# A fused attention and two-expert-stage kernel whose second stage forms y w1 by one level of Strassen's recursion

## The chip, the cores and the metric

One core of a Trainium2 chip runs one program. The metric is device time in microseconds (us) from the program's first to its last instruction, as the median of timed runs; smaller is better. The engines are TensorE (PE, with its weight loads as PEld), VectorE (DVE), ScalarE (ACT), GpSimd (POOL) and the DMA queue of SyncE (SP).

## What the kernel must compute

Attention in chunks makes x (1536 tokens by 512). A gated block turns x into another 1536 by 512 matrix, called y here, and four experts then work on every token:

```python
def _moe_ref(x, w_gate, w_val, w_out):
    gate = 1.0 / (1.0 + np.exp(-(x @ w_gate)))
    return gate * (x @ w_val) @ w_out                 # 512 -> 1536 -> 512

def _moe2_ref(x, domain_probs, w1, w2):               # x here is y; w1 is [4, 512, 1024], w2 [4, 1024, 512]
    p = domain_probs / (domain_probs.sum(-1, keepdims=True) + 1e-09)
    for e in range(4):
        h = np.maximum(x @ w1[e], 0.0)
        out += p[:, e:e + 1] * (h @ w2[e])
```

Every float32 operand of a large product is split into hi + lo, each exact in float32r, and a product is three matmuls: hi hi, hi lo and lo hi.

## The kernel before

The program has one order, written out by hand for each engine; nothing is rescheduled. It has three stages. In the first, attention is made in blocks of 384 tokens, with pieces of x w_val between its steps; TensorE's matmuls for these write a tile named pv of 384 columns. In the second, x w_gate (tile pg) and the rest of x w_val are made in steps of 512 tokens, and then the product with w_out: for each of three 512-token steps four PSUM tiles pb, one for each 128 columns of y, stand open at once, and for each of 12 pieces of the inner dimension every one of them gets three matmuls. ACT and DVE then split pb into the four y tiles ys (hi and lo, all 1536 tokens). During the third of these steps they also split the first expert's w1.

The third stage is the experts. For each expert and each 512-token step, h_unit (line 481) is called 8 times: 12 matmuls of 512 columns (4 pieces of the inner dimension by 3) add up in one PSUM tile ph, ACT writes the relu's hi part and DVE its lo part. Then o_unit (line 493) is called for 4 groups of 128 tokens: 24 matmuls of 512 columns (8 by 3) add up in a PSUM tile po, and DVE multiplies it by the expert's weight of each token and adds it to acc, one SBUF tile for each of the 12 token groups. The last token group is made in two halves of 256 columns, so that less is left behind the last matmul. The helper mm3 (line 160) issues every one of these triples, so their rows stand on lines 161 to 163 and are told apart by their tiles.

PSUM has 8 banks, given out in turn by ps_tile. Weights come by DMA on SP's queue into four raw tiles of 512 KB (rawp), from which ACT (hi) and DVE (lo) write them into 12 places (wp) for w1 and 10 (wp2) for w2.

## Time and profile before

| | |
|---|---|
| median of 3 runs | 893.57 us (892.66 to 893.98) |
| span of the profiled execution | 893.9 us |
| TensorE busy, share of the span | 870.0 us, 97% |
| DVE, ACT, POOL busy | 315.1, 231.4 and 18.8 us |
| mean granted TensorE clock | 0.996 |

The profiled execution has no time of its own beside its span; the span is 0.3 us above the median and inside the range of the runs, so no offset stands between them. A busy TensorE is one with a matmul in flight: the matmuls overlap, so a matmul's own duration (0.39 us for 512 columns) is longer than the distance from one start to the next, and it is that distance that adds up to the time.

### The profile page before, as it was taken

The page shows a single profiled execution, that of the slowest core. Times are in us where ns is not written, and L with a number is a line of the kernel's source. Part 1 is how long each engine was busy: PE and PEld are TensorE (multiplying, and loading weights), DVE is VectorE, ACT ScalarE, POOL GpSimd, SP SyncE. Part 2 cuts the span into 40 slices and gives each one's busy share as a digit, 9 for nine tenths or more (in the row PEclk, how much of TensorE's full clock was granted, in tenths as well). Part 3 has the DMA queues.
Part 4 walks back from the last instruction along what each step waited for, and adds up shares of the span by engine and source line. Part 5 has one row for each costly group of instructions (what it writes and reads, how often), then busy time and mean ns, then how long its engine had stood idle before and what let it go on. Part 6 is the DMA issues. An engine that isn't in the chain of part 4 may idle for free.

```text
span 893.9 us, 10956 instructions
## 1 busy us (share of the span) xinstructions
PE 870.0 (97%) x4607; PEld 723.7 (81%) x4607; DVE 315.1 (35%) x550; ACT 231.4 (26%) x479; POOL 18.8 (2%) x23
## 2 busy tenths in 40 slices
PE   6689999999999999999999999999999999999998
PEld 3578998888888888888888888888888888888887
DVE  5565366652453334331114322123322123412121
ACT  4455445432232334321112211012201012302020
POOL 2211000000000000000000000000000000000000
PEclk9999999999999999999999999999999999999999
DMA  9999333320220002120002110002110002000101
GB/s 216 246 253 252 102 99 118 114 65 30 71 71 23 1 1 71 47 71 1 1 0 88 51 52 1 0 1 95 48 47 1 1 1 95 0 36 12 48 0 48
DMA packets 19168, 55.35 MB, mean 62 GB/s; under 512 B 2592, under 2 KB 4912, under 8 KB 19120
## 3 DMA queue, kind: packets, MB, share of 16 engines
q1 hardware_dynamic: 19088, 54.63, 21.3%
q8 instruction: 36, 0.59, 0.3%
q14 instruction: 12, 0.10, 0.0%
q0 software_dynamic: 32, 0.02, 0.0%
HBM read 51.50 MB, written 3.15 MB: 61 GB/s over the span
## 4 chain that ended last, share of the span: by engine, by line
PE 91%; DMA 8%; SPq 1%; issue 0%; DVE 0%
PE po L161 10%; PE po L163 10%; PE po L162 10%; PE ph L161 10%; PE ph L162 10%; PE ph L163 10%; DMA kb<-in_kw_dram 4%; PE pb L163 4%; PE pb L161 4%; PE pb L162 4%; PE pg L163 4%; PE pg L161 4%; PE pg L162 4%; PE pv L161 3%; PE pv L163 3%; PE pv L162 3%
## 5 line engine op out<-in xcount | busy, mean ns | idle before, releaser
L488 ACT ACTIVATE h<-ph 128x512 fp32r<-128x512 f32 x96 | 57.4, 598 | 414.4 <-PE ph L163 414.4
L163 PE MATMUL po<-w,h 128*128 128x512 f32 (+1 forms) x392 | 151.0, 385 | 0.0
L162 PE MATMUL po<-w,h 128*128 128x512 f32 (+1 forms) x392 | 151.0, 385 | 0.0
L161 PE MATMUL po<-w,h 128*128 128x512 f32 (+1 forms) x392 | 151.0, 385 | 0.0
L163 PE MATMUL ph<-ys,w 128*128 128x512 f32 x384 | 149.6, 390 | 0.0
L161 PE MATMUL ph<-ys,w 128*128 128x512 f32 x384 | 149.6, 389 | 0.0
L162 PE MATMUL ph<-ys,w 128*128 128x512 f32 x384 | 149.6, 389 | 0.0
L489 DVE SCALAR_TENSOR_TENSOR h<-ph,h 128x512 fp32r<-128x512 f32 x96 | 66.4, 692 | 184.3 <-ACT h L488 184.3
L161 PEld LDWEIGHTS po<-w,h 128*128 128x128 f32 x392 | 73.7, 188 | 14.7
L163 PEld LDWEIGHTS po<-w,h 128*128 128x128 f32 x392 | 73.7, 188 | 14.7
L162 PEld LDWEIGHTS po<-w,h 128*128 128x128 f32 x392 | 73.7, 188 | 14.6
L163 PEld LDWEIGHTS ph<-ys,w 128*128 128x128 f32 x384 | 72.1, 188 | 15.0
L161 PEld LDWEIGHTS ph<-ys,w 128*128 128x128 f32 x384 | 72.1, 188 | 15.0
L162 PEld LDWEIGHTS ph<-ys,w 128*128 128x128 f32 x384 | 72.1, 188 | 14.9
L505 DVE SCALAR_TENSOR_TENSOR acc<-po,p_sb,acc 128x512 f32<-128x512 f32 (+1 forms) x37 | 27.2, 736 | 152.3 <-PE po L163 152.3
L161 PE MATMUL pv<-xs,w_v 128*128 128x384 f32 (+1 forms) x176 | 64.1, 364 | 0.2 <-ACT g L317 0.2
L163 PE MATMUL pv<-xs,w_v 128*128 128x384 f32 (+1 forms) x176 | 61.8, 351 | 0.0
L162 PE MATMUL pv<-xs,w_v 128*128 128x384 f32 (+1 forms) x176 | 61.6, 350 | 0.0
L163 PE MATMUL pb<-hl,w_o 128*128 128x512 f32 x144 | 57.1, 397 | 0.0
L161 PE MATMUL pb<-hl,w_o 128*128 128x512 f32 x144 | 57.1, 397 | 0.0
L162 PE MATMUL pb<-hl,w_o 128*128 128x512 f32 x144 | 57.1, 397 | 0.0
L163 PE MATMUL pg<-xs,w_g 128*128 128x512 f32 x144 | 56.1, 390 | 0.0
(72 smaller groups left out, 910.1 us busy)
## 6 DMA issues: line engine op xcount, KB each, us to landing
raw<-in_w_dram SPq DMA_DIRECT2D x32, 512.0 KB, 3.5
vb<-in_vw_dram SPq DMA_DIRECT2D x32, 195.0 KB, 7.9
kb<-in_kw_dram SPq DMA_DIRECT2D x32, 192.0 KB, 7.6
raw<-in_w_v_dram SPq DMA_DIRECT2D x12, 512.0 KB, 8.6
raw<-in_w_g_dram SPq DMA_DIRECT2D x12, 512.0 KB, 4.4
raw<-in_w_o_dram SPq DMA_DIRECT2D x12, 512.0 KB, 3.4
q<-in_qT_dram SPq DMA_DIRECT2D x16, 192.0 KB, 7.3
out_dram<-acc SPq DMA_DIRECT2D x11, 256.0 KB, 2.0
```

What stands on the lines that cost most here:

```text
L161: nc.tensor.matmul(out=ps, lhsT=w_hi, rhs=r_hi, start=first, stop=False)
L162: nc.tensor.matmul(out=ps, lhsT=w_hi, rhs=r_lo, start=False, stop=False)
L163: nc.tensor.matmul(out=ps, lhsT=w_lo, rhs=r_hi, start=False, stop=last)
L488: nc.scalar.activation(out=h[:, 0], in_=ps, func=AF.Relu)
L489: nc.vector.scalar_tensor_tensor(out=h[:, 1], in0=ps, scalar=0.0, in1=f32(h[:, 0]), op0=ALU.max, op1=ALU.subtract)
L505: nc.vector.scalar_tensor_tensor(out=a, in0=ps[:, n], scalar=p, in1=a, op0=ALU.mult, op1=ALU.add)
```

## The change

The product y w1 of each expert is made by one level of Strassen's recursion (in Winograd's form). The quarters of y are 384 tokens by 256, those of w1 are 256 by 256, and seven products of sums of quarters take the place of eight. Tokens go in two rounds of 768, and w1 and w2 in 16 pieces: a block is one round with one half of an expert's w1 and w2. There are 16 blocks (15 loads of a piece: the round change keeps its piece), and each has two units (128 of the 256 columns of the quarters). A unit makes seven products of 6 matmuls of 384 columns in three PSUM tiles b, e and a: some products add to a tile whose earlier value ACT has just copied out (held), and DVE adds such copies to later tiles (total) to get three of the four quarters of h; the fourth is made in finish, later. Then the block's second product runs as 12 parts of 6 matmuls of 512 columns into six PSUM tiles d; the last part of a block is put into the next block's first unit (prev).

The sums of w1's quarters are made on POOL, in place in the raw tiles (w1_prep: 4 sums), and ACT and DVE split seven tiles of 512 columns for a piece of w1 and four for a piece of w2. They are issued in steps (hooks) between the parts of the block before. The sums of y's quarters are made on POOL too (y_sums), and seven splits of 768 columns follow for each round (y_prep, y_prep_late).

```diff
-    def mm3(ps, w_hi, w_lo, r_hi, r_lo, first, last):
-        nc.tensor.matmul(out=ps, lhsT=w_hi, rhs=r_hi, start=first, stop=False)
-        nc.tensor.matmul(out=ps, lhsT=w_hi, rhs=r_lo, start=False, stop=False)
-        nc.tensor.matmul(out=ps, lhsT=w_lo, rhs=r_hi, start=False, stop=last)
+    def mm3(ps, w_hi, w_lo, r_hi, r_lo, first, last, more=False):
+        nc.tensor.matmul(out=ps, lhsT=w_hi, rhs=r_hi, start=first, stop=False, skip_group_check=more)
+        nc.tensor.matmul(out=ps, lhsT=w_hi, rhs=r_lo, start=False, stop=False, skip_group_check=more)
+        nc.tensor.matmul(out=ps, lhsT=w_lo, rhs=r_hi, start=False, stop=last, skip_group_check=more)
...
+    blocks = [(0, e, g) for e in range(NE) for g in range(NGR)]
+    blocks += [(1, e, g) for e in reversed(range(NE)) for g in reversed(range(NGR))]
+    groups = [b[1:] for b in blocks[:NE * NGR]] + [b[1:] for b in blocks[NE * NGR + 1:]]
+    group_of = [n if n < NE * NGR else n - 1 for n in range(len(blocks))]
...
+    def in_turn(splits):
+        his, los = zip(*splits)
+        return [his[0]] + [both(h, l) for h, l in zip(his[1:], los)] + [los[-1]]
...
+    def w1_prep(n):
+        t = {}
...
+        def hi(m, a):
+            def do():
+                w = wp.tile([128, 2, 2, GW], F32R, tag="w", name=f"w1_{n}_{m}")
+                ops1[n][m] = w
+                nc.scalar.copy(out=w[:, 0], in_=t[a])
+            return do
...
+        def lo(m, a):
+            def do():
+                w = ops1[n][m]
+                nc.vector.tensor_tensor(out=w[:, 1], in0=t[a], in1=f32(w[:, 0]), op=ALU.subtract)
+            return do
+        def comb(dst, a, b, op):
+            return lambda: nc.gpsimd.tensor_tensor(out=t[dst], in0=t[a], in1=t[b], op=op)
...
+        s1 = comb("a22", "a21", "a22", ALU.add)
+        s3 = comb("a21", "a11", "a21", ALU.subtract)
+        s2 = comb("a11", "a22", "a11", ALU.subtract)
+        s4 = comb("a12", "a12", "a11", ALU.subtract)
+        return [
+            both(start, hi(4, "a22"), hi(1, "a11")), both(lo(4, "a22"), s1), both(hi(2, "a12"), lo(1, "a11"), s3, s2),
+            both(lo(2, "a12"), s4), hi(7, "a21"), both(hi(6, "a11"), lo(7, "a21")), both(hi(5, "a22"), lo(6, "a11")),
+            both(hi(3, "a12"), lo(5, "a22")), both(lo(3, "a12"), lambda: raw1_to(n + 3))]
...
+        h, l = ([fn(u, fh) for u in range(2) for fh in range(2)] for fn in (hi, lo))
+        return [both(h[0], h[1], l[0]), both(h[2], l[1]), l[2], h[3], l[3]]
...
+    def y_sums(j, into, eng):
+        y = yr[j]
+        q = {(k, t): y[:, 2 * k:2 * k + 2, t * HT:(t + 1) * HT] for k in range(2) for t in range(2)}
+        d = {(k, t): into[:, 2 * k:2 * k + 2, t * HT:(t + 1) * HT] for k in range(2) for t in range(2)}
+        t1, t3, t2, t4 = d[0, 0], d[0, 1], d[1, 1], d[1, 0]
+        sub = ALU.subtract
+        return (q, dict(t1=t1, t3=t3, t2=t2, t4=t4), dict(
+            t1=combine(eng, t1, q[0, 1], q[0, 0], sub), t3=combine(eng, t3, q[1, 1], q[0, 1], sub),
+            t2=combine(eng, t2, q[1, 1], t1, sub), t4=combine(eng, t4, q[1, 0], t2, sub)))
...
+        def start():
+            q, t, do = y_sums(j, yr[j], nc.gpsimd)
+            h1, l1 = y_split(1, q[0, 0])
+            h3, l3 = y_split(3, q[1, 1])
+            h2, l2 = y_split(2, q[1, 0])
+            h5, l5 = y_split(5, t["t1"])
+            h7, l7 = y_split(7, t["t3"])
+            h6, l6 = y_split(6, t["t2"])
+            h4, l4 = y_split(4, t["t4"])
+            out.extend([
+                [h1], [h3, l1, do["t1"], do["t3"]], [h2, l3, do["t2"]], [h5, l2, do["t4"]],
+                [h7, l5], [h6, l7], [h4, l6], [l4]])
...
+    def y_prep_late(j):
+        q, t, _ = y_sums(j, yr[0], nc.gpsimd)
+        return in_turn([
+            y_split(1, q[0, 0]), y_split(7, t["t3"]), y_split(6, t["t2"]), y_split(2, q[1, 0]),
+            y_split(4, t["t4"]), y_split(5, t["t1"]), y_split(3, q[1, 1])])
...
+        def product(n, u, m, ps, first):
+            w, y = ops1[group_of[n]][m], yops[0][m]
+            fc = slice(u * 128, (u + 1) * 128)
+            for k in range(2):
+                mm3(ps[:, :HT], w[:, 0, k, fc], w[:, 1, k, fc], y[:, 0, k], y[:, 1, k], first and k == 0, k == 1,
+                    not first)
...
+        def total(name, ps, s):
+            v = small(name, 4)
+            nc.vector.tensor_tensor(out=v, in0=ps[:, :HT], in1=s, op=ALU.add)
+            return v
+        def held(ps):
+            s = small("s", 6)
+            nc.scalar.copy(out=s, in_=ps[:, :HT])
+            return s
...
+        def unit(n, u, prev):
+            b, e = ps_tile(f"b{n}_{u}"), ps_tile(f"e{n}_{u}")
+            product(n, u, 1, b, True)
+            s1 = held(b)
+            product(n, u, 7, e, True)
+            s7 = held(e)
+            a = None
+            if prev is None:
+                a = ps_tile(f"a{n}_{u}")
+                product(n, u, 2, a, True)
+            else:
+                prev()
+            product(n, u, 6, b, False)
+            s2 = held(b)
+            if a is None:
+                a = ps_tile(f"a{n}_{u}")
+                product(n, u, 2, a, True)
+            hook()
+            c11 = total("v", a, s1)
+            h_hi(n, u, (0, 0), c11)
+            product(n, u, 4, e, False)
+            c21 = total("v", e, s2)
+            h_lo(n, u, (0, 0), c11)
+            h_hi(n, u, (1, 0), c21)
+            product(n, u, 5, b, False)
+            c22 = total("v", b, s7)
+            h_lo(n, u, (1, 0), c21)
+            h_hi(n, u, (1, 1), c22)
+            h_lo(n, u, (1, 1), c22)
+            hook()
+            def finish():
+                product(n, u, 3, b, False)
+                h_hi(n, u, (0, 1), b[:, :HT])
+                h_lo(n, u, (0, 1), b[:, :HT])
+            return finish
...
+        def o_part(n, d, tt, u, first, last, cols):
+            th, c = divmod(tt, RT // 2)
+            c = slice(c * 128, (c + 1) * 128)
+            for fh in range(2):
+                h, w = H2[n, u, (fh, th)], ops2[group_of[n], u, fh]
+                mm3(d[:, cols], h[:, 0, c], h[:, 1, c], w[:, 0, cols], w[:, 1, cols],
+                    first and fh == 0, last and fh == 1)
+                hook(keep=2)
...
+        for n in range(len(blocks)):
+            end = n == len(blocks) - 1
+            if n == 2:
+                for do in y_sums(1, yr[0], nc.gpsimd)[2].values():
...
+            fin0 = unit(n, 0, prev)
+            if n == 0:
+                hook(2)
+            fin1 = unit(n, 1, fin0)
+            hook(len(hooks))
+            if n == NE * NGR - 1:
+                hooks.extend(y_prep_late(1))
+            elif not end:
+                g = group_of[n + 1]
+                hooks.extend(w1_prep(g) + w2_prep(g))
+            ds, waiting = {}, []
+            def part(tt, u, d_first=0, d_last=1):
...
+            part(0, 0)
+            part(1, 0)
+            fin1()
+            part(2, 0)
+            part(3, 0)
+            part(0, 1)
+            part(1, 1)
+            flushed(0)
+            part(2, 1)
+            flushed(1)
+            part(3, 1)
+            flushed(2)
+            part(4, 0)
+            flushed(3)
+            part(4, 1)
+            if not end:
+                part(5, 0)
+                flushed(4)
...
+                def prev(n=n, ds=ds):
+                    o_part(n, ds[5], 5, 1, False, True, ALL)
+                    flush(n, ds[5], 5, ALL)
+            else:
...
+                if c == NCT - 1:
+                    y_steps, w_steps = y_prep(0), w1_prep(0)
                 for f in range(KF):
...
-                    if c == NCT - 1 and n_w < n_64 + KE:
-                        split_f32(wp, n_w)
-                        n_w += 1
+                    if c == NCT - 1:
+                        emit(y_steps, 1)
+                        emit(w_steps, 1 if f >= 2 else 0)
...
+                    yr.extend(xp.tile([128, KD, 2 * HT], F32, tag="x", name=f"yr{j}") for j in range(NR))
+                    yops.extend(y_ops())
                 for m in range(KD):
-                    if c == 0:
-                        y_t[m] = xp.tile([128, 2, B * S], F32R, tag="x", name=f"ys{m}")
-                    put_split(y_t[m][:, 0, ct(c)], y_t[m][:, 1, ct(c)], pss[m])
...
+                    for j in range(NR):
+                        t0, t1 = max(c * CT, j * 2 * HT), min((c + 1) * CT, (j + 1) * 2 * HT)
+                        if t0 < t1:
+                            nc.scalar.copy(
+                                out=yr[j][:, m, t0 - j * 2 * HT:t1 - j * 2 * HT], in_=pss[m][:, t0 - c * CT:t1 - c * CT])
```

Place 1, TensorE. The first expert unit. In the kernel before, the twelve matmuls of a tile ph stand together; four of them from the second tile on, with their y tiles ys:

```order
L163 MATMUL ph0_0_0_3359<-ys3_2921,w_1_0_0_3135 128x512
L161 MATMUL ph0_0_1_3378<-ys0_2912,w_1_0_1_3153 128x512
L162 MATMUL ph0_0_1_3378<-ys0_2912,w_1_0_1_3153 128x512
L163 MATMUL ph0_0_1_3378<-ys0_2912,w_1_0_1_3153 128x512
L161 MATMUL ph0_0_1_3378<-ys1_2915,w_1_0_1_3153 128x512
```

In the changed kernel, at the end of block 0's first unit (b0_0, e0_0: PSUM tiles of block 0, unit 0; yo4, yo5, yo1: operands made from y; w1_0_5: the fifth product's operand made from w1):

```order
L152 MATMUL e0_0_3381<-yo4_2924,w1_0_4_3180 128x384
L150 MATMUL b0_0_3380<-yo5_2925,w1_0_5_3298 128x384 [waits Activation_49]
L151 MATMUL b0_0_3380<-yo5_2925,w1_0_5_3298 128x384
L152 MATMUL b0_0_3380<-yo5_2925,w1_0_5_3298 128x384 [waits DVE_49]
L150 MATMUL b0_0_3380<-yo5_2925,w1_0_5_3298 128x384
L151 MATMUL b0_0_3380<-yo5_2925,w1_0_5_3298 128x384
L152 MATMUL b0_0_3380<-yo5_2925,w1_0_5_3298 128x384
L150 MATMUL b0_1_3451<-yo1_2919,w1_0_1_3182 128x384 [waits PE_49]
```

A tile changes every 6 matmuls instead of every 12, the tile b0_0 is one that matmuls had written before, and the matmul that returns to it waits for ACT (the copy held).

Place 2, ACT. In the kernel before, in the second token step of the first expert, ACT has one relu for each tile ph and nothing between them:

```order
L488 ACTIVATE h0_1_0_3636<-ph0_1_0_3623 128x512 [waits PE_49]
L488 ACTIVATE h0_1_1_3652<-ph0_1_1_3639 128x512 [waits DVE_49,PE_49]
L488 ACTIVATE h0_1_2_3668<-ph0_1_2_3655 128x512 [waits DVE_49,PE_49]
L488 ACTIVATE h0_1_3_3684<-ph0_1_3_3671 128x512 [waits DVE_49,PE_49]
L488 ACTIVATE h0_1_4_3700<-ph0_1_4_3687 128x512 [waits DVE_49,PE_49]
```

In the changed kernel, from the second product of block 0 to the first unit of block 1 (w1_1_4: fourth product's operand of piece 1, w2_1_0_0: a piece of w2, s: the copies held):

```order
L223 CAST w1_1_2_3542<-raw1_1_0_2912 128x512
L361 ACTIVATE h0_1_(0, 1)_3558<-b0_1_3451 128x384 [waits PE_49]
L223 CAST w1_1_7_3565<-raw1_1_1_2914 128x512 [waits Pool_49]
L223 CAST w1_1_6_3570<-raw1_1_0_2912 128x512 [waits Pool_49]
L223 CAST w1_1_5_3577<-raw1_1_1_2914 128x512
L223 CAST w1_1_3_3583<-raw1_1_0_2912 128x512 [waits Pool_49]
L251 CAST w2_1_0_0_3597<-raw2_1_0_3494 128x512 [waits DMAHW4_49]
L251 CAST w2_1_0_1_3599<-raw2_1_1_3496 128x512 [waits DMAHW5_49]
L251 CAST w2_1_1_0_3605<-raw2_1_0_3494 128x512
L375 COPY s_3657<-b1_0_3649 128x384 [waits PE_49,Activation_49]
```

Three splits now wait for POOL, and the copy that TensorE waits for stands behind them.

Place 3, POOL. In the kernel before its last tensor work is in the first stage. In the changed kernel these rows are the four sums of one piece of w1, each in place in a raw tile:

```order
L233 TENSOR_TENSOR raw1_1_1_2914<-raw1_1_1_2914 128x512 [waits DMAHW3_49,DMAHW7_49,DMAHW2_49,DVE_49]
L233 TENSOR_TENSOR raw1_1_1_2914<-raw1_1_0_2912,raw1_1_1_2914 128x512 [waits DMAHW6_49,Pool_49]
L233 TENSOR_TENSOR raw1_1_0_2912<-raw1_1_1_2914,raw1_1_0_2912 128x512 [waits DMAHW2_49,DVE_49,Pool_49]
L233 TENSOR_TENSOR raw1_1_0_2912<-raw1_1_0_2912 128x512 [waits DVE_49,Pool_49]
```

They follow each other as a chain: each one after the first waits for POOL's own earlier sum, and the first waits for DVE, which has to have read the raw tile.

## Rows read from the trace of the kernel before

**Rows 1.** The page's first part: busy time, share of the span, instructions.
```profile
PE 870.0 (97%) x4607; PEld 723.7 (81%) x4607; DVE 315.1 (35%) x550; ACT 231.4 (26%) x479; POOL 18.8 (2%) x23
```

**Rows 2.** Busy time of each engine by stretch, granted clock, DMA share, GB/s.
```profile
core 0: us, PE busy (x) PEld busy (x) DVE busy (x) ACT busy (x) POOL busy (x), PEclk, DMA share, GB/s
...
119.83:136.12 16.29, 16.29 (x95) 16.29 (x95) 15.05 (x29) 10.13 (x20) 0.00 (x0) 1.00 0.54 161
136.12:266.72 130.60, 130.60 (x577) 108.16 (x577) 64.61 (x109) 45.64 (x79) 0.00 (x0) 1.00 0.24 77
266.72:368.16 101.44, 101.44 (x434) 81.67 (x433) 38.58 (x59) 31.57 (x54) 0.00 (x0) 1.00 0.08 26
368.16:890.69 522.53, 522.49 (x2328) 433.62 (x2326) 136.73 (x202) 86.67 (x153) 0.00 (x0) 1.00 0.09 30
```

**Rows 3.** The page's chain that ended last, by engine.
```profile
PE 91%; DMA 8%; SPq 1%; issue 0%; DVE 0%
```

**Rows 4.** Groups of TensorE's matmuls by tile and shape: count, busy, mean ns.
```profile
L163 PE MATMUL ph<-ys,w 128*128 128x512 f32 x384 | 149.6, 390 | 0.0
...
L163 PE MATMUL po<-w,h 128*128 128x512 f32 x376 | 146.5, 390 | 0.0
...
L163 PE MATMUL pb<-hl,w_o 128*128 128x512 f32 x144 | 57.1, 397 | 0.0
...
L162 PE MATMUL po<-w,h 128*128 128x256 f32 x16 | 4.5, 284 | 0.0
```

**Rows 5.** TensorE's instructions in order of time: start us, us.
```profile
119.83 0.33 PE L163 MATMUL pv<-xs,w_v 128*128 128x384 f32 x1
...
120.35 0.33 PE L163 MATMUL pv<-xs,w_v 128*128 128x384 f32 x1
...
136.12 0.39 PE L161 MATMUL pg<-xs,w_g 128*128 128x512 f32 x1
...
266.72 0.40 PE L161 MATMUL pb<-hl,w_o 128*128 128x512 f32 x1
...
367.93 0.39 PE L161 MATMUL ph<-ys,w 128*128 128x512 f32 x1
...
846.66 0.39 PE L161 MATMUL ph<-ys,w 128*128 128x512 f32 x1
...
868.42 0.39 PE L161 MATMUL po<-w,h 128*128 128x512 f32 x1
...
884.74 0.28 PE L161 MATMUL po<-w,h 128*128 128x256 f32 x1
...
890.38 0.28 PE L163 MATMUL po<-w,h 128*128 128x256 f32 x1
```

**Rows 6.** Groups of ACT's instructions by shape: count, busy, mean ns, idle before.
```profile
L111 ACT CAST w<-raw 128x512 fp32r<-128x512 f32 x64 | 37.3, 615 | 13.4 <-PE pb L163 13.4
...
L317 ACT COPY g<-pv 128x384 f32<-128x384 f32 x32 | 15.1, 484 | 30.7 <-PE pv L163 30.5
```

**Rows 7.** The same of DVE.
```profile
L112 DVE TENSOR_TENSOR w<-raw,w 128x512 fp32r<-128x512 f32 x64 | 42.0, 684 | 12.2 <-ACT w L111 12.2
...
L505 DVE SCALAR_TENSOR_TENSOR acc<-po,p_sb,acc 128x512 f32<-128x512 f32 x35 | 26.3, 750 | 147.8 <-PE po L163 147.8
...
L302 DVE TENSOR_TENSOR xs<-x,xs 128x384 fp32r<-128x384 f32 x16 | 8.9, 554 | 10.3 <-ACT xs L298 10.3
```

**Rows 8.** The same of POOL.
```profile
L144 POOL TENSOR_TENSOR w_v<-t,w_v 128x512 fp32r<-128x512 f32 x8 | 10.4, 1303 | 60.5 <-ACT w_v L132 60.5
```

**Rows 9.** DMA issues: count, KB each, median us from issue to landing.
```profile
raw<-in_w_dram SPq DMA_DIRECT2D x32, 512.0 KB, 3.5
```

**Rows 10.** DVE in order of time, the last row.
```profile
890.69 0.48 DVE L505 SCALAR_TENSOR_TENSOR acc<-po,p_sb,acc 128x256 f32<-128x256 f32 x1 [2.39 <-PE po L163]
```

More of the change, by code (lines that the diff above doesn't have):

```diff
@@ L35 @@
 RAWS = 4
+HT = 384
+NR = B * S // (2 * HT)
+RT = 2 * HT // 128
+NGR = 2
+GW = FE // 2 // NGR
 TICKS = (0, 0, 1, 1, 1, 1, 1, 0, 1, 1, 1, 1, 1, 0, 1, 0, 0)
@@ L88, in fused_kernel @@
     n_64 = len(order)
-    for e in range(NE):
-        order += [("1", e, f) for f in range(KE)]
-        order += [("2", e, f) for f in range(KE)]
     src = {"g": w_g, "v": w_v, "o": w_o}
@@ L169, in ct, with raw1_to @@
         return slice(c * CT, (c + 1) * CT)
+    blocks = [(0, e, g) for e in range(NE) for g in range(NGR)]
+    blocks += [(1, e, g) for e in reversed(range(NE)) for g in reversed(range(NGR))]
+    groups = [b[1:] for b in blocks[:NE * NGR]] + [b[1:] for b in blocks[NE * NGR + 1:]]
+    group_of = [n if n < NE * NGR else n - 1 for n in range(len(blocks))]
+    yr, yops, raw1, raw2s = [], [], {}, {}
+    ops1, ops2 = {}, {}
+    pools = {}
+    def raw1_to(n):
+        for i in range(len(raw1), min(n, len(groups))):
+            raw1[i] = []
+            for fh in range(2):
+                r = rawp.tile([128, KD, GW], F32, tag="raw", name=f"raw1_{i}_{fh}")
+                nc.sync.dma_start(out=r, in_=w_1[groups[i][0], groups[i][1], fh])
+                raw1[i].append(r)
@@ new lines, in raw2_to, with put_hi, put_lo @@
+    def raw2_to(n):
+        for i in range(len(raw2s), min(n, len(groups))):
+            raw2s[i] = []
+            for fh in range(2):
+                r = pools["raw2"].tile([128, 2, DM], F32, tag="raw2", name=f"raw2_{i}_{fh}")
+                nc.sync.dma_start(out=r, in_=w_2[groups[i][0], groups[i][1], fh])
+                raw2s[i].append(r)
+    def put_hi(dst, src):
+        return lambda: nc.scalar.copy(out=dst, in_=src)
+    def put_lo(dst, hi, src):
+        return lambda: nc.vector.tensor_tensor(out=dst, in0=src, in1=f32(hi), op=ALU.subtract)
@@ new lines, in combine, with both @@
+    def combine(eng, dst, a, b, op):
+        return lambda: eng.tensor_tensor(out=dst, in0=a, in1=b, op=op)
+    def both(*parts):
+        return lambda: [p() for p in parts]
+    def in_turn(splits):
[4 more added lines that the diff above has]
+        def start():
+            raw1_to(n + 1)
+            r0, r1 = raw1[n]
+            t.update(a11=r0[:, :2], a12=r0[:, 2:], a21=r1[:, :2], a22=r1[:, 2:])
+            ops1[n] = {}
+        def hi(m, a):
[19 more added lines that the diff above has]
+            both(hi(3, "a12"), lo(5, "a22")), both(lo(3, "a12"), lambda: raw1_to(n + 3))]
@@ new lines, in w2_prep, with hi, do, lo @@
+    def w2_prep(n):
+        def hi(u, fh):
+            def do():
+                raw2_to(n + 1)
+                w = pools["wp2"].tile([128, 2, DM], F32R, tag="w2", name=f"w2_{n}_{u}_{fh}")
+                ops2[n, u, fh] = w
+                nc.scalar.copy(out=w[:, 0], in_=raw2s[n][fh][:, u])
+            return do
+        def lo(u, fh):
+            def do():
+                w = ops2[n, u, fh]
+                nc.vector.tensor_tensor(out=w[:, 1], in0=raw2s[n][fh][:, u], in1=f32(w[:, 0]), op=ALU.subtract)
+                if (u, fh) == (1, 1):
+                    raw2_to(n + 2)
+            return do
+        h, l = ([fn(u, fh) for u in range(2) for fh in range(2)] for fn in (hi, lo))
+        return [both(h[0], h[1], l[0]), both(h[2], l[1]), l[2], h[3], l[3]]
@@ new lines, in y_ops @@
+    def y_ops():
+        op = {}
+        for ms in ((1, 7), (6, 2)):
+            tl = xp.tile([128, 2, 2, 2, HT], F32R, tag="x", name=f"yo{ms[0]}")
+            for q, m in enumerate(ms):
+                op[m] = tl[:, q]
+        pool = tc.alloc_tile_pool(name="yo", bufs=1, side="right", reuse_waits="tile")
+        pools["yo"] = pool
+        for m in (4, 5, 3):
+            op[m] = pool.tile([128, 2, 2, HT], F32R, name=f"yo{m}")
+        return [op]
+    def y_sums(j, into, eng):
[7 more added lines that the diff above has]
+            t2=combine(eng, t2, q[1, 1], t1, sub), t4=combine(eng, t4, q[1, 0], t2, sub)))
@@ new lines, in y_split, with y_prep, start, step @@
+    def y_split(m, src):
+        op = yops[0][m]
+        return put_hi(op[:, 0], src), put_lo(op[:, 1], op[:, 0], src)
+    def y_prep(j):
+        out = []
+        def start():
+            q, t, do = y_sums(j, yr[j], nc.gpsimd)
[9 more added lines that the diff above has]
+                [h7, l5], [h6, l7], [h4, l6], [l4]])
+        def step(i):
+            def do():
+                if i == 0:
+                    start()
+                for p in out[i]:
+                    p()
+            return do
+        return [step(i) for i in range(8)]
```

136 lines of the change are left out of this document (69 added, 67 removed).

## The prediction

> **What bounds the kernel now.** I read the page's busy times first: TensorE has a matmul in flight for 870.0 of 893.9 us; its weight loads (81%) run beside that, and no other engine passes 35% [rows 1]. The stretches say where it idles: only before 119.83 us. From there on its busy time fills each stretch, to 522.49 of 522.53 us in the experts' stage, at a granted clock of 1.00 [rows 2]; the chain that ended last is 91% TensorE [rows 3]. So in the stage that is changed the time is the number of matmuls times the distance between their starts, and nothing else is on the path until the last accumulation [rows 10].
>
> That distance is read from first rows of runs that have no gap [rows 5]. 96 matmuls of ph (8 calls of 12) lie between 846.66 and 868.42: 21.76 / 96 = 0.2267 us. 72 of po (3 calls of 24) lie between 868.42 and 884.74: 0.2267 us too. 48 halves of 256 columns: 47 steps from 884.74 to 890.38, 0.120 us. For 384 columns the rows of pv give three steps in 0.52 us, 0.1733 us, and the whole run up to 136.12 fits 94 such steps. The three lie on a line: 128 columns more cost 0.0533 us, and each matmul has 0.0133 us beside its columns.
>
> **The reading holds.** The experts' stage has 1152 matmuls of ph, 1128 whole and 48 half ones of po [rows 4] (three lines each): 261.1 + 255.7 + 5.8 = 522.6 us. It runs from 367.93 to about 890.5 [rows 5]: 522.6 us. The count times the distance gives the stage to 0.1 us.
>
> **The matmuls removed and added.** Each of 16 blocks has two units of seven products of 6 matmuls: 16 x 2 x 7 x 6 = 1344 of 384 columns at 0.1733 = 232.9 us, in place of 261.1 us: -28.2. (The columns' own part, 261.1 less 1152 x 0.0133, is 245.8 us and falls by an eighth, 30.7; 192 more matmuls pay 0.0133 us each, 2.6, back.) The second product keeps its columns: 16 x 72 = 1152 matmuls, of which now only the last 12 are made as 24 halves: 1140 x 0.2267 + 24 x 0.120 = 261.3 instead of 261.4, -0.1. Sum: **-28.3 us**.
>
> The Trainium skill, "TensorE: Matmul & The Clock Gate", section "Back-to-back issue gap", gives the gap as columns / 2.4 + 2.5 ns, and adds that pairs with weight loads behave otherwise. By it the products would fall from 248.6 to 218.4 us, 30.2 less; the rows differ from it (226.7 against 215.8 ns), and the measurement decides.
>
> **What must stay hidden.** Per block TensorE works 84 x 0.1733 + 72 x 0.2267 = 30.9 us. Beside it:
> - ACT: 6 copies and 8 relus of 384 columns at 0.484, 11 splits of 512 at 0.615 [rows 6]: 13.5 us.
> - DVE: 6 totals and 8 lo parts of 384 at 0.554, 11 splits at 0.684, 6 accumulations at 0.750 [rows 7]: 19.8 us, where before it had 136.73 us in the whole stage [rows 2]; 16 blocks make 316.
> - POOL: 4 sums at 1.303 [rows 8]: 5.2 us.
> - DMA: four loads of 512 KB, each landing in 3.5 us [rows 9].
>
> None passes 64% of the block, so only order can make TensorE wait. DVE's and ACT's weight has no price on the distance itself: with DVE busy half of the time in the stretch from 136.12 (64.61 of 130.60) 576 matmuls of 512 columns (577 counted, one begun before) take 130.60 us, again 0.2267 [rows 2, 5].
>
> Three waits could show, and I follow each by its queue. First, a product that adds to b needs ACT's copy: it is 0.484 long and the next product into b starts at least two products (2.08 us) later. Covered. Second, finish writes b again and needs DVE's third total. Between the end of product 5 and finish lie two products of the next unit, 2.08 us; DVE has at most what is left of the second total and one lo part before it, and ends the third total some 0.6 us after product 5. Covered by 1.4 us; after the second unit two parts (2.72 us) lie there.
>
> Third, the chain of weight preparation. Count from the end of product 5 of the second unit. DVE owes two lo parts and the first split of w1: 2 x 0.554 + 0.684, and with the third total in front about 2.4 us. Then four sums on POOL, one behind the other (5.2), the last split on ACT (0.6), three splits of w2 (1.85): about 10.1 us. Behind them on ACT stands the copy of b, 0.5 us, and TensorE wants it when it has made 11 parts (15.0), finish (1.0), two products and the part put in between (3.4): 19.4 us. Some 9 us to spare. Cost 0. What is not covered is the start of round two: there the lo part of the third product's y (768 columns, by the two DVE rows an estimate of 0.554 + 3 x 0.130 = 0.94 us) comes behind two lo parts of h and is wanted by finish's second matmul at 2.25 us: 0.6 + 1.1 + 0.94 = 2.65, and I take **+0.6** with the hand-overs, once.
>
> At the start of the stage y's seven splits and w1's seven ride in the last step of the product with w_out (33.8 us, a third of 101.2 [rows 5]): ACT 12 x 0.615 + 7 splits of 768 columns (about 0.85 each by its two rows) + 7 x 0.615, 17.6 us; POOL four sums of 768 columns (1.5 times 1.303) and four of 512: 13 us. They fit; the copies into yr cost ACT what the splits into ys did. On SP's queue the first load of w2 stands behind loads that wait for DVE to give a raw tile back, some 5 us before the stage; should it land as late as 3.5 us into the stage, ACT's split of it holds up relus whose result is wanted only by the first part, 14 products (14.6 us) in. Later loads are issued a block (30.9 us) ahead. Cost 0. The first four PSUM tiles of the stage wait for TensorE itself; the row's length over its distance is 0.39 - 0.2267, so between 0 and 0.16 us each, and I take **+0.3**.
>
> **The unknown.** The product with w_out ran slower: 432 matmuls of 512 columns (three lines of 144 [rows 4]) in 367.93 - 266.72 = 101.21 us, 0.2343 each, 7.6 ns over ph [rows 5]. What it has of its own is that it returns to one of four open tiles every three matmuls; ph stays 12 in a tile and po 24, at equal distance, so fresh tiles cost nothing. The new code stays 6, and often returns to a tile written before. No row shows six. Below, nothing; above: 3 x 7.6 = 23 ns for each return (four products a unit and six parts a block, 224 in all) is 5.2 us, for every change of tile (416) 9.6 us, and 7.6 ns on all 2508 matmuls 19.1 us. I take 0, because 12 and 24 do not differ at all; if a change cost were spread over them, ph would be 1 ns over po. The other bounds stay for the range.
>
> The end is as before: half a tile's accumulation and its store [rows 10].
>
> **Sum.** -28.3 + 0.6 + 0.3 = -27.4 us, from the span 893.9 to 866.5; against the median, 893.57 to **866.2 us**.
>
> **Rivals.**
> 1. Short groups pay. For: pb's rows. Against: ph and po alike. By returns 866.2 + 5.2 = 871.4, by every change 875.8. If all matmuls ran at pb's distance, 885.3.
> 2. The weight preparation holds TensorE up, and the kernel becomes slower. The place is the copy of b behind ACT's splits that wait for POOL. With a sum of P us the chain is 5.3 + 4 P against 19.4, so it decides from P = 3.5, and 14 blocks with a preparation lose the 27.4 us from 3.5 + 27.4 / 14 / 4 = 4.0 us a sum: there 893.6, at 4.2 us 904. Against it stands the row's 1.303; for it speaks only that POOL now works beside a DVE at 64%. The Trainium skill, "GPSIMD Engine Reference", section "Engine selection", advises against GpSimd for elementwise work of two inputs, at about twice VectorE's time; the rows agree (1.303 against 0.684 us), and twice is not the three times that this needs.
> 3. What a matmul pays beside its columns does not grow with their number in the new stream: then the columns' 30.7 us stay whole and the time is 866.2 - 2.5 = 863.7. Against it: 256, 384 and 512 columns all pay 13.3 ns. The skill's formula above lies on this side (30.2).
> 4. One of the covered waits is not covered: 0.1 us on each of 32 units is 3.2 us, 869.4.
> That the change does not do what it says can be left out: the order has the 1344 matmuls of 384 columns.
>
> **How the numbers follow.** Forecast (865 to 868): 0.70. Rival 1: 0.14, of which 0.03 for pb's distance throughout. Rival 2: 0.05, of which 0.04 end slower than before and 0.01 near it. Rival 3: 0.02. Rival 4: 0.09. The range 863.5 to 876 holds the forecast, rival 4 and most of rival 1, and leaves about 0.1 out. A measurement of this kernel tells 0.2% (1.8 us) from no change: faster 0.95, same 0.01, slower 0.04.
>
> **What would show it.** Right: in the experts' stage TensorE's starts 0.1733 us apart in products and 0.2267 in parts, busy time equal to the stretch, its length about 495 us, and one gap of half a us at the start of round two. Wrong: distances over these in products that return to b (rival 1); waits of TensorE for ACT's copies with POOL rows of 3 us and more (rival 2); small waits for DVE's totals in each unit (rival 4).

## The result, and the profile after

The changed kernel takes 871.44 us, median of 4 runs (869.25 to 871.61), against 893.59 of the kernel before (4 runs, 892.66 to 893.98): 0.9743 of it, 95% interval 0.9725 to 0.9761. It is faster, by 22.2 us where 27.4 were forecast.

The profiled execution has a span of 869.8 us and a time of its own of 871.6. In every run whose time and span are both known, of either kernel, the time stands 1.7 to 2.2 us above the span, so the two are not one figure, as was taken ahead of the prediction: the execution of before that the prediction read, span 893.9, was itself some 2 us over its median. What differs most between executions lies ahead of the gated projections: these begin between 131.7 and 139.3 us in the twelve later profiles, since TensorE waits there for loads of the attention (19.7 us in this one). Below, stretches behind that point are compared, from start to start of TensorE's matmuls; those that an edit did not touch repeat to 0.1 us.

First the page's busy times and chain, which answer to [rows 1, 3].

```profile
PE 843.2 (97%) x4787; PEld 741.0 (85%) x4787; DVE 514.2 (59%) x829; ACT 351.8 (40%) x726; POOL 129.7 (15%) x91
...
PE 87%; DMA 8%; DVE 3%; SPq 1%; ACT 1%; issue 0%; DVEq 0%; ACTq 0%
```

TensorE is still the path. DVE and ACT, hardly on it before, have some 4% together. The stretches answer to [rows 2], with the same columns: gated projections, product with w_out, experts' stage.

```profile
135.84:266.44 130.60, 130.60 (x577) 108.11 (x577) 64.61 (x109) 45.66 (x79) 0.00 (x0) 1.00 0.23 77
266.44:366.23 99.79, 98.52 (x433) 80.93 (x432) 46.72 (x54) 36.46 (x63) 15.03 (x8) 1.00 0.05 17
366.23:866.53 500.30, 499.18 (x2509) 452.02 (x2507) 327.93 (x486) 202.12 (x391) 95.94 (x60) 1.00 0.18 63
```

The gated projections have not moved. The product with w_out, whose instructions on TensorE the change does not touch, is 1.4 us shorter (99.79 against 101.21), although TensorE now idles in it. The experts' stage is 22.5 us shorter. TensorE's waits from there on, and where they stand in order of time (start, us, and in brackets the idle time and what ended it):

```profile
PE pb L151 <- DVE hl L109: 1.1, 1, 1.1
PE b L150 <- ACT s L375: 0.6, 1, 0.6
PE b L151 <- DVE yo L196: 0.5, 1, 0.5
```

```profile
366.23 0.33 PE L150 MATMUL b<-yo,w 128*128 128x384 f32 x1
...
375.51 0.34 PE L152 MATMUL b<-yo,w 128*128 128x384 f32 x1
376.44 0.45 PE L150 MATMUL b<-yo,w 128*128 128x384 f32 x1 [0.59 <-ACT s L375]
376.73 0.34 PE L151 MATMUL b<-yo,w 128*128 128x384 f32 x1
...
624.69 0.34 PE L150 MATMUL b<-yo,w 128*128 128x384 f32 x1
625.49 0.45 PE L151 MATMUL b<-yo,w 128*128 128x384 f32 x1 [0.47 <-DVE yo L196]
...
866.20 0.28 PE L152 MATMUL d<-w,h_(1, 1)_7494 128*128 128x256 f32 x1
```

From first to last start the stage lasts 866.20 - 366.23 = 499.97 us. The number of matmuls times the distance between their starts is 1344 x 0.1733 + 1140 x 0.2267 + 23 x 0.12 = 494.12 ("count times distance" below). Of the 5.85 us over it, the two waits are 1.61: a start that comes 0.93 us after the one before it in place of 0.17 and the next 0.29 in place of 0.17, then 0.80 and 0.28. The other 4.24 us are no waits. They are matmuls that start some ns late, the same ones in every block. The groups by tile and shape (busy, mean ns of one | idle before) show which:

```profile
L152 PE MATMUL pb<-hl,w_o 128*128 128x512 f32 x144 | 56.0, 389 | 0.0
L150 PE MATMUL e<-yo,w 128*128 128x384 f32 x128 | 43.1, 337 | 0.0
L150 PE MATMUL a<-yo,w 128*128 128x384 f32 x64 | 21.4, 334 | 0.0
```

pb has gone from 397 to 389 ns, ph's 390 of before [rows 4]. e, which holds products 7 and 4, is longer than a, which holds product 2 alone.

### The profile page after: what moved, and what is told of

It is laid out like the page before. It is cut to its first block, busy times and chain, and to the rows that moved or that the text cites. A ratio compares the mean times of both kernels' runs of the same rounds, so it can differ in the third digit from the quotient of the medians.

```text
span 869.8 us, 12089 instructions
## 1 busy us (share of the span) xinstructions
PE 843.2 (97%) x4787; PEld 741.0 (85%) x4787; DVE 514.2 (59%) x829; ACT 351.8 (40%) x726; POOL 129.7 (15%) x91
## 4 chain that ended last, share of the span: by engine, by line
PE 87%; DMA 8%; DVE 3%; SPq 1%; ACT 1%; issue 0%; DVEq 0%; ACTq 0%
PE d L152 10%; PE d L151 10%; PE d L150 10%; PE b L151 5%; PE b L150 5%; PE b L152 5%; PE pg L152 4%; PE pg L150 4%; PE pg L151 4%; DMA kb<-in_kw_dram 4%; PE pb L151 3%; PE pb L152 3%; PE pb L150 3%; PE pv L150 3%; PE pv L151 3%; PE pv L152 3%
## 5 line engine op out<-in xcount | busy, mean ns | idle before, releaser
L229 DVE TENSOR_TENSOR w<-raw,w 128x512 fp32r<-128x512 f32 x105 | 107.0, 1062 | 21.2 <-ACT w L223 19.3
L233 POOL TENSOR_TENSOR raw<-raw 128x512 f32<-128x512 f32 x30 | 49.5, 1648 | 373.5 <-DVE w L229 372.4
L432 DVE SCALAR_TENSOR_TENSOR acc<-d,p_sb,acc 128x512 f32<-128x512 f32 (+1 forms) x85 | 58.6, 734 | 59.2 <-PE d L152 59.2
L150 PE MATMUL b<-yo,w 128*128 128x384 f32 x256 | 86.5, 338 | 0.6 <-ACT s L375 0.6
L151 PE MATMUL b<-yo,w 128*128 128x384 f32 x256 | 86.5, 338 | 0.5 <-DVE yo L196 0.5
L152 PE MATMUL b<-yo,w 128*128 128x384 f32 x256 | 86.4, 337 | 0.0
L375 ACT COPY s<-b 128x384 f32<-128x384 f32 x64 | 30.4, 475 | 134.6 <-PE b L152 134.6
L223 ACT CAST w<-raw 128x512 fp32r<-128x512 f32 x105 | 60.7, 617 | 43.4 <-POOL raw L233 43.4
L152 PE MATMUL pg<-xs,w_g 128*128 128x512 f32 x144 | 56.0, 389 | 0.0
L151 PE MATMUL pg<-xs,w_g 128*128 128x512 f32 x144 | 56.0, 389 | 0.0
L150 PE MATMUL pg<-xs,w_g 128*128 128x512 f32 x144 | 56.0, 389 | 0.0
L109 DVE TENSOR_TENSOR hl<-g,hl 128x512 fp32r<-128x512 f32 x36 | 27.1, 754 | 48.9 <-ACT hl L108 48.9
L654 ACT ACTIVATE sg<-pg 128x512 f32<-128x512 f32 x36 | 21.5, 598 | 83.5 <-PE pg L152 83.5
L150 PEld LDWEIGHTS b<-yo,w 128*128 128x128 f32 x256 | 48.1, 188 | 2.8 <-ACT s L375 0.9
L151 PEld LDWEIGHTS b<-yo,w 128*128 128x128 f32 x256 | 48.1, 188 | 2.7 <-DVE yo L196 0.8
```

The lines of the kernel that those rows point to most:

```text
L109: nc.vector.tensor_tensor(out=lo, in0=src, in1=f32(hi), op=ALU.subtract)
L150: nc.tensor.matmul(out=ps, lhsT=w_hi, rhs=r_hi, start=first, stop=False, skip_group_check=more)
L151: nc.tensor.matmul(out=ps, lhsT=w_hi, rhs=r_lo, start=False, stop=False, skip_group_check=more)
L152: nc.tensor.matmul(out=ps, lhsT=w_lo, rhs=r_hi, start=False, stop=last, skip_group_check=more)
L223: nc.scalar.copy(out=w[:, 0], in_=t[a])
L229: nc.vector.tensor_tensor(out=w[:, 1], in0=t[a], in1=f32(w[:, 0]), op=ALU.subtract)
```

## The experiments

**Why do some matmuls start late?** A matmul reads two operands from SBUF; below, the one given as lhsT is the stationary operand (the weight load) and the one given as rhs the moving operand. The prediction looked for the cause of pb's longer distance in its return to open PSUM tiles (its rival 1; theory B). But the changed kernel's product 6 returns to a tile at no cost, product 4 pays, and pb got faster with its order kept. What had changed for pb is where hl lies in SBUF. The addresses that the built program gives led to theory A: a moving operand that does not start at a multiple of 64 bytes pays. The first four runs, with their edits in short:

```diff
+ if i == 0: hlp.tile([128, 8], F32, tag="pad")    # hl_to_64: 3 x 32 bytes ahead of hl
+ if i == 0: hlp.tile([128, 16], F32, tag="pad")   # hl_by_192: 3 x 64 bytes
+ pool.tile([128, 8], F32, name="pad")             # yo_to_64: in the pool of yo4, yo5, yo3
+ pad of 32 bytes ahead of wp2, and of hp          # w2_off_64, on top of yo_to_64
```

> The kernel before, with 96 bytes of padding ahead of the three buffers of hl, the moving operand of the product with w_out; these then start at 206144, a multiple of 64 bytes, instead of 206048, which is 32 over one (addresses in each partition, as the built program has them). The order of the products, with its return to one of four open PSUM tiles every three matmuls, stays. Theory A (a moving operand that starts off a multiple of 64 bytes costs some ns per matmul): pb's distance falls from 0.2343 to 0.2267 us, 432 of them are 3.3 us, so 890.3 us. Theory B (the return to open tiles costs, as the prediction supposed): the distance stays 0.234 and the time 893.6.

> As the run before, but with 192 bytes of padding: hl starts at 206240, moved farther, and again 32 over a multiple of 64. Theory A: nothing changes, pb at 0.2343 us, 893.6. Theory C (another place in SBUF, or any move, is what helped): the distance falls here too. Theory B: no change in either.

> The changed kernel, with 32 bytes of padding in the pool of yo4, yo5 and yo3, which then start at 210880, 217024 and 223168 (multiples of 64) instead of 32 over. Theory A: products 4, 5 and 3 (192 groups of 6 matmuls, 3.5 ns each over the 173.3 of the other products) come to 173.3 ns, 4.0 us of 1152 matmuls at most, some 3 us by what their rows have over; 868 to 869 us. Theory B: these products stay slow, since their groups and their tiles are the same, 871.4.

> The run before, with 32 bytes ahead of the pool of w2, the moving operand of the second product, and 32 more behind its raw tiles, so that h and acc keep to multiples of 64. Theory A: 1140 matmuls of 512 columns take 0.2343 instead of 0.2267 us, 8.7 us more than the run before. Theory B: no change.

The first matmul of pb and of the stage behind it, of hl_to_64, then of hl_by_192:

```profile
268.02 0.39 PE L161 MATMUL pb<-hl,w_o 128*128 128x512 f32 x1
...
365.94 0.39 PE L161 MATMUL ph<-ys,w 128*128 128x512 f32 x1
```

```profile
269.86 0.40 PE L161 MATMUL pb<-hl,w_o 128*128 128x512 f32 x1
...
370.67 0.40 PE L161 MATMUL ph<-ys,w 128*128 128x512 f32 x1
```

97.92 us for 432 matmuls are 0.2267 each; 100.81 are 0.2334. So 96 bytes of padding take away what rival 1 would have charged to the PSUM tiles, and 192 bytes give most of it back, with the order of products untouched: theory B falls, and theory C (any move helps) with it. In time hl_to_64 is 891.07 us against 894.12 of before beside it, 0.9968 (0.9947 to 0.9988). The single time of hl_by_192, 898.49, lies above by a late start (its gated projections begin at 139.26).

w2_off_64 (877.21 us, one run) agrees with A in kind: the stage of 505.45 us is 6.46 longer than that of yo_to_64, 5.7 ns by 1140 matmuls (8.7 us were expected). But yo_to_64 contradicts it. Its stage, 498.99 us, is 1.0 shorter where some 3 were expected, and most of that lies in the second product, whose operands had not moved; product 4 keeps its 3.5 ns, product 5 has 2.7 of its 3.3. Here e of yo_to_64, then e of the later run yo_to_256:

```profile
L152 PE MATMUL e<-yo,w 128*128 128x384 f32 x128 | 43.1, 337 | 0.0
```

```profile
L152 PE MATMUL e<-yo,w 128*128 128x384 f32 x128 | 42.8, 334 | 0.0
```

The time of yo_to_64, 870.76 us (866.53 to 873.32; 0.9728, 0.9684 to 0.9772), cannot be told from the changed kernel's. What the undisturbed cases had in common was not a multiple of 64, but the distance from the moving operand to the stationary one: theory D. The next runs:

```diff
+ pool.tile([128, 40], F32, name="pad")            # yo_to_256: 160 bytes in yo's pool
+ const.tile([128, 8], F32, name="pad0")           # all_by_32: all of the left side moves by 32, yo too (its pad is 128 bytes)
+ pad of 32 bytes ahead of hp, and of accp         # h_off_32, on top of yo_to_256
```

> The changed kernel, with 160 bytes of padding in the pool of yo4, yo5 and yo3: they start at 210752, 216896 and 223040, 64 over a multiple of 256 as all other operands of TensorE do (w, xs, yo1, yo6, w2, h, hl). Theory D (what costs is the distance in SBUF between the moving operand and the stationary one: nothing where it is a multiple of 256 bytes, some ns of each matmul where it is not): products 4, 5 and 3 come to 173.3 ns, and the experts' stage from 5.85 to about 3.0 us over count times distance. Theory A (multiples of 64 alone): no change against yo_to_64, 4.9 us over. Theory B (groups and returns): 4.9 to 5.9 us over, the products stay slow.

> As yo_to_256, but with 32 bytes of padding ahead of the weights' pool, so that every operand of TensorE starts 96 over a multiple of 256: none is at a multiple of 64, and all distances between operands are kept. Theory D: no change against yo_to_256, pb at 0.2267 us and the second product at 0.2267. Theory A: pb, the gated projections and the second product all run at 0.233 to 0.234, and the products at 0.177, 20 us more in all.

> As yo_to_256, but with 32 bytes ahead of the pool of h alone, the stationary operand of the second product; its moving one, w2, stays where it was. Theory D: 1140 matmuls of 512 columns pay 6 to 8 ns, 7 to 9 us more. Theory A (the moving operand's own start): no change.

First and last matmul of the experts' stage, of all_by_32, then of h_off_32:

```profile
363.47 0.33 PE L151 MATMUL b<-yo,w 128*128 128x384 f32 x1
...
861.93 0.28 PE L153 MATMUL d<-w,h_(1, 1)_7496 128*128 128x256 f32 x1
```

```profile
367.75 0.33 PE L150 MATMUL b<-yo,w 128*128 128x384 f32 x1
...
872.17 0.27 PE L152 MATMUL d<-w,h_(1, 1)_7503 128*128 128x256 f32 x1
```

498.46 us for all_by_32, as for yo_to_256 (367.66 to 866.12): with no operand at a multiple of 64, nothing is lost, and A falls. h_off_32 moves only the stationary operand and pays 504.42 - 498.46 = 5.96 us, where 7 to 9 were expected. That is 5.2 ns by 1140 matmuls, but the stage also holds changes of width (below), whose price was not the same in both. Inside a long run of parts, where no change is near, 36 distances between starts show it alone, of h_off_32, then of yo_to_256:

```profile
483.24 0.40 PE L150 MATMUL d<-w,h_(0, 0)_4314 128*128 128x512 f32 x1
...
491.64 0.40 PE L150 MATMUL d<-w,h_(0, 1)_4294 128*128 128x512 f32 x1
```

```profile
481.87 0.39 PE L150 MATMUL d<-w,h_(0, 0)_4306 128*128 128x512 f32 x1
...
490.03 0.39 PE L150 MATMUL d<-w,h_(0, 1)_4286 128*128 128x512 f32 x1
```

8.40 us against 8.16, 0.2333 each against 0.2267: 6.6 ns, inside the 6 to 8 expected. In w2_off_64 the same places are 0.2333 apart too. D stands. The cases together, by the programs' addresses in bytes in each partition and the remainder of their distance by 256 (product 4's cost by the mean distance of e's starts, half of which are product 7's; the second product's inside long runs of parts):

```
                          moving - stationary   remainder     ns over 226.7 (173.3)
pb, before                206048 -   5184           160          7.6
pb, hl_by_192             206240 -   5184            96          6.7
pb, hl_to_64              206144 -   5184             0          0.0
pb, changed kernel        193600 -   5184             0          0.0 (but for waits)
2nd product, h_off_32     135232 - 172128           224          6.6
2nd product, w2_off_64    135264 - 172160           224          6.6
product 4, changed        210912 -   5184           160          3.5
product 4, yo_to_64       210880 -   5184           128          3.5
product 4, yo_to_256      210752 -   5184             0          0.0
```

By the same addresses all other float32r matmuls of the two kernels (pv, pg, ph, po, products 1, 7, 6 and 2, parts) lie at remainder 0.

The times of these three runs (871.55, 867.34 and 877.6 us, one each) scatter with the start of the gated projections (137.3, 133.1 and 137.4). yo_to_256 took 1.5 of the 4.24 us, not the 2.85 expected. Products 4 and 5 gave 1.3 of it, all that they had; product 3 stands behind a change of width and loses as much there as before. 2.67 us stay, nearly all in the 6 to 10 matmuls behind the 93 changes between 512 and 384 columns.

**Where is the edge of rival 2?** Extra sums on GpSimd lengthen the chain of weight preparation.

```diff
  def comb(dst, a, b, op):
+     for twice in (add, subtract):        # sums_x2: for two of the four sums only
+         gpsimd.tensor_tensor(out=t[dst], in0=t[dst], in1=t[other], op=twice)
      gpsimd.tensor_tensor(out=t[dst], in0=t[a], in1=t[b], op=op)
```

> The changed kernel; each sum of GpSimd over a quarter of w1 has two more of its kind ahead of it, one that adds and one that takes off again, so that 12 sums stand in the chain in place of 4 (values but for rounding as before). By the prediction's second rival the chain is 5.3 us and 12 sums of 1.65, 25.1 us, against 19.4, 5.7 us late in each of 14 blocks: 80 us more. By the trace of the changed kernel 8 more sums are 13.2 us against some 7.8 of slack at the first copy of the next block: 5.4 us late, 76 us more. Against both: if the weights are ready a block ahead anyway, nothing changes.

> As sums_x3, but only two of the four sums have the two extra ones ahead: 8 in the chain. Tripled sums held TensorE up by 3.7 us net at the first product that adds to b, with 8 more sums of some 1.5 us, so the slack of the copy is about 8 us. Four more sums are 6 us: no wait, and the experts' stage as in the changed kernel, 500 us from first to last matmul. By the prediction's sum (5.3 + 8 x 1.65 = 18.5 against 19.4) no wait either. If the slack were that of another reader (the first PSUM tiles, the second or third product), a wait of 1 us or more would show in each block.

sums_x3 took 970.1 us (one run, as sums_x2). Its wait, with the next two matmuls, and the stretch behind it (PEclk is the third figure from the end):

```profile
PE b L150 <- ACT s L380: 50.7, 15, 3.6
```

```profile
639.44 0.69 PE L150 MATMUL b<-yo,w 128*128 128x384 f32 x1 [3.58 <-ACT s L380]
639.93 0.52 PE L151 MATMUL b<-yo,w 128*128 128x384 f32 x1
640.25 0.52 PE L152 MATMUL b<-yo,w 128*128 128x384 f32 x1
```

```profile
639.93:645.05 5.12, 5.12 (x17) 5.12 (x17) 4.48 (x8) 1.52 (x3) 0.00 (x0) 0.50 0.56 184
```

The place is that of rival 2: the copy of b behind ACT's splits. It is late in 14 blocks; the 15th wait is block 0's, as in the changed kernel. The 180 sums average 1.45 us; by the prediction's formula 12 of them are 17.4, 5.3 + 17.4 = 22.7 against 19.4, 3.3 us late, and the start came 3.8 us late. What the rival lacked is what follows a wait: starts 0.32 us apart at a granted clock of 0.50, which is 384 columns at 1.2 GHz in place of 2.4, so that a block lost some 6.4 us and not 3.8. The kernel took 98.7 us more than the changed kernel, where 76 to 80 were expected: by the stretches some 52 are these waits, 35 the slow clock behind them, 5 one more wait in block 2, and 7 a longer pb. The 8 added sums are 11.6 us, so the slack was 11.6 - 3.8 = 7.8 us, where the prediction had 9. With 4 added (sums_x2, 881.88 us), 5.8 us, no block behind block 0 has this wait. But my expectation of an unchanged stage missed one place. In block 2, where the sums for round two come as well, DVE's accumulations are late once:

```profile
440.48 0.69 PE L150 MATMUL a<-yo,w 128*128 128x384 f32 x1 [4.63 <-DVE acc L437]
```

With the slow clock behind it that is nearly all of the 7.1 us by which its stage is longer (507.05 us). The longer pb, 4.2 us in sums_x2 and 6.8 in sums_x3, was not expected either. It tests what sums on GpSimd do to DVE, whose instructions are the same as in the changed kernel. The same split of hl, of the changed kernel, then of sums_x3, where a sum now runs beside it:

```profile
357.28 0.68 DVE L109 TENSOR_TENSOR hl<-g,hl 128x512 fp32r<-128x512 f32 x1
```

```profile
359.43 1.76 DVE L109 TENSOR_TENSOR hl<-g,hl 128x512 fp32r<-128x512 f32 x1
```

**Can the rest be had?** Three versions, on top of yo_to_256.

```diff
- tile_pool(name="hl", bufs=3)      + bufs=4, and g_split(i + 3)        # waits_gone
-     hook(2)                       +     hook(1)                       #   block 0
-     hook(keep=2)                  +     hook(keep=0 if n == 7 else 2)
- products 1, 7, prev part, 6, 2, 4, 5; finish between parts            # products_together:
+ products 1, 7, 6, 2, 5, 4, 3; then all twelve parts
+ unit 0: 1, 7, 6, 2, 5, 4; unit 1: 1, 7, 6, 3 of unit 0, 5, 2, 4, 3    # third_later
+ if n or u: hook()                                                     #   block 0
```

> As yo_to_256, and each of the three places where TensorE waited is given more room: four buffers of hl, split three steps ahead in place of two; one split of w2 less before the second unit of the first block; the last two splits of y for round two made in the second product of block 7 and not in block 8. Of the changed kernel's profile 1.8 us in pb, 0.9 us at 376 and 0.7 us at 625 go, and 1.5 us by the place of yo: 4.9 us less than the changed kernel, 866.5. If the waits come back elsewhere (DVE has no room in the last step of the product with w_out), 868 to 870.

> As waits_gone, and the products of a block follow each other without parts of the second product between them: in each unit 1, 7, 6, 2, 5, 4, 3 (5 ahead of 4, so that its total is ready when 3 adds to the same tile), and all twelve parts behind them. The width of the matmuls then changes twice in a block, not six times. Theory E (a change of width costs 26 ns from 512 to 384 columns and 43 ns the other way, spread over the next 6 to 10 matmuls): 16 blocks x about 105 ns, 1.7 us less than waits_gone, 864.8. If one product does not cover a copy or a total (it lasts 1.04 us; a total is 0.55 us, a copy 0.48), a wait shows in each of 32 units: 0.3 us there would be 10 us more.

> As products_together, but the third product has two products between it and the total that it waits for: that of a block's first unit comes in the second unit behind product 6, that of the second unit behind product 4, with 5 ahead of 2 and 4 there; and no split of w2 stands in the first unit of block 0, where its load was late. Of the small losses in products_together (1.95 us over count times distance) half stood at product 3 of each unit, without a change of width: 26 ns, as behind a change. Theory E (the change of width itself costs): these 26 ns stay, 1.9 us. Theory F (a matmul that reaches its semaphore just as it is given loses the lead of its weight load, and a change of width does the same): they go, 1.1 us stay. In both the waits of 2.5 us go or fall under 0.5, so the experts' stage is 495.7 to 496.5 us against 497.3 of waits_gone and 498.6 of products_together.

waits_gone: 868.05 us (5 runs, 866.19 to 868.61), 0.9689 (0.9665 to 0.9714) of the 895.41 of before beside it. pb falls to 97.92 us, all of its 1.87 us of lateness gone; the stage is 497.28, with one pair of starts left that comes 0.45 us late. That is 4.5 us less than the changed kernel from pb on, where 4.9 were expected. products_together: 865.99 us (6 runs, 864.30 to 869.94), 0.9675 (0.9646 to 0.9704). Its stage, 498.57 us, is longer by 1.3 and not shorter by 1.7. The small losses fall only to 1.95 us for 32 changes of width, because product 3 of each unit now loses 26 ns without a change; and two waits appear, in blocks 0 and 2. The first of them, then that of third_later's block 2:

```profile
368.43 0.34 PE L152 MATMUL e<-yo,w 128*128 128x384 f32 x1
369.96 0.44 PE L150 MATMUL b<-yo,w 128*128 128x384 f32 x1 [1.20 <-DVE v L371]
```

```profile
435.97 0.45 PE L150 MATMUL b<-yo,w 128*128 128x384 f32 x1 [0.88 <-ACT s L376]
```

third_later: 867.02 us (5 runs, 866.18 to 869.64), 0.9693 (0.9669 to 0.9716). The 26 ns at product 3 went, and 1.15 us of small losses stay: theory F's number, not E's 1.9. But its stage is 498.76 us (362.71 to 861.47), since new one-time waits that cost 3.5 us together stand in blocks 0 and 2, and my bound for these fell. All three versions beat the changed kernel: each was timed beside the kernel before, and their intervals lie below its 0.9725 to 0.9761. By their times they cannot be told apart, by the stretches behind the start waits_gone is the best.

## Why the prediction was right in kind and 3.5 us off in size

From the gated projections to the last matmul the profiles give 754.25 before (136.12 to 890.38) and 730.36 after (135.84 to 866.20): 23.9 us. The medians differ by 22.2, with 21.4 to 24.6 in the interval. Against the 27.4 of the forecast that is 3.5 us off by the stretches and 5.2 by the medians. The measured 871.44 lies inside the stated range of 863.5 to 876, but outside the 865 to 868 that had a chance of 0.70. That 871.4 is also what rival 1 gave for its returns is chance: the parts of the sum are others. In part luck, too, is how near the total came: a gain of 3.3 us and losses of 7.0 that no term held stand against each other.

- **The matmuls removed and added**, -28.3: right. Where nothing disturbs them, products start 0.1733 us apart and parts 0.2267, and returns to a tile cost nothing (products 4 and 5 in yo_to_256). Rival 3 falls, rival 1 by its mechanism.
- **The unknown**: this is the first step that went wrong. The 0 that it took for returns and short groups was right. The distance of pb was real, but its cause was another: hl lay 160 bytes off a multiple of 256 from w_o. The change moved hl as a side effect of a pool (tp) that went to the other end of SBUF, and pb gained 3.3 us, which no term held. The same cause cost the experts' stage 1.5 us, nearly all in products 4 and 5, and changes of width 2.7, where the step took 0.
- **What must stay hidden**, start of the stage: the second step that went wrong. It added up ACT and POOL for the last step of the product with w_out, and not DVE, and it took durations from rows in which DVE and POOL did not run side by side. DVE, then POOL, in order of time in that step:

```profile
342.48 2.61 DVE L196 TENSOR_TENSOR yo<-yr,yo 128x768 fp32r<-128x768 f32 x1
345.01 0.68 DVE L229 TENSOR_TENSOR w<-raw,w 128x512 fp32r<-128x512 f32 x1
345.62 2.33 DVE L109 TENSOR_TENSOR hl<-g,hl 128x512 fp32r<-128x512 f32 x1
347.87 2.05 DVE L196 TENSOR_TENSOR yo<-yr,yo 128x768 fp32r<-128x768 f32 x1
349.84 1.78 DVE L229 TENSOR_TENSOR w<-raw,w 128x512 fp32r<-128x512 f32 x1
```

```profile
342.13 2.15 POOL L199 TENSOR_TENSOR yr<-yr 128x768 f32<-128x768 f32 x1 [0.98 <-DVE yo L196]
345.26 2.14 POOL L199 TENSOR_TENSOR yr<-yr 128x768 f32<-128x768 f32 x1 [0.99 <-DVE yo L196]
347.36 1.75 POOL L233 TENSOR_TENSOR raw<-raw 128x512 f32<-128x512 f32 x1
```

  One piece (f) of this step gives TensorE 12 x 0.2267 = 2.72 us; a split of hl that took 0.68 alone took 2.33 beside POOL. hl came late, 1.9 us in all. (By the prediction's own rows DVE's work adds up to 19.6 of the step's 33.8 us, an estimate, so the sum over the whole step would have passed it too.) ACT's splits of w2 held up a copy of b in block 0 for another 0.87; the prediction saw these splits and thought of the relus behind them, not of the copy.
- **Start of round two**, +0.6: right, 0.74, at the place named. The **first four PSUM tiles**, +0.3: no such wait shows. In waits_gone the lateness of hl and of round two is gone and that of block 0 half gone, so that these waits were the cost is shown by experiment, not only read; that POOL's sums slow DVE's splits, by sums_x3.
- **Rival 2**: its place was right, its slack nearly (9 against 7.8 us), its price too low. Rival 4 did not occur: no unit waits as a rule.

The sum as it came out: -28.3 - 3.3 + 1.9 + 0.9 + 0.7 + 1.5 + 2.7 = -23.9 us.

## What to carry to other kernels

When one stage runs a few ns per matmul slower than another of the same shape, compare the SBUF addresses of its moving and stationary operands before its order: 96 bytes of padding were worth 3% of the product with w_out here, and 32 bytes in the wrong place cost 1% of the experts' stage. Add up every engine for the shortest interval that has to repeat, not for the stage, and with durations taken beside the engines that will run then. A move of an unrelated pool can change a stage that the diff never mentions, so compare all stretches, the untouched ones first.

## What the runs showed of the hardware that was not expected

- Matmuls of 512 columns with float32r operands started 226.7 ns apart when moving and stationary operand lay a multiple of 256 bytes apart, and 6.6 to 7.6 ns later at remainders of 96, 160 and 224; of 384 columns, 3.5 ns later at 128 and 160. Other remainders were not run. The Trainium skill, "SBUF — State Buffer", section "Who interferes with whom", gives TensorE two independent read ports, for the moving operand and for the weight load, and says that it never waits on anyone; by these runs its pace still depends on where the two operands lie, and the measurement decides. Which part of the chip makes them meet is open.
- Behind a change of width TensorE lost up to 26 ns (512 to 384 columns) or 38 to 47 ns (384 to 512), spread over the next matmuls; 26 ns also appeared without one, where a total was given just as product 3 came to its turn, and went when it was given earlier. That both come from a weight load that loses its lead was only argued.
- DVE's subtraction of two SBUF tiles went from 0.68 to 2.33 us beside GpSimd's sums, and GpSimd's sum from 1.30 [rows 8] to between 1.53 and 1.89 in the same step. Of the changed kernel's 201 splits of hl, w1 and w2, the 134 without a sum beside them took at most 0.69 us, and the 67 beside one 1.36 on the mean. The Trainium skill, "SBUF — State Buffer", section "Who interferes with whom", says that a DVE instruction with two SBUF inputs contends with a GpSimd one that reads SBUF; the trace agrees.
- In sums_x3 the granted clock fell to 0.50 at or just behind the waits of 3.58 us in all 14 blocks, and starts of 384 columns came 0.32 us apart, 1.2 GHz in place of 2.4. In sums_x2 it fell likewise behind the wait of 4.63 us, and in pb behind one of 2.19 us for hl. Behind the changed kernel's waits of up to 1.1 us it stayed at 1.00. In sums_x3 this added some two thirds to what the waits cost.
